# Block-sparse attention with a mixture of experts on one core: the first loads spread over two issuing engines

## The chip, the core and the metric

The kernel runs on one core of one Trainium2 chip. A core has five engines that run side by side, each with its own instruction queue in order: TensorE (PE in the profile, with PEld for its weight loads), VectorE (DVE), ScalarE (ACT), GpSimd (POOL) and SyncE (SP), which here issues loads and stores. Loads and stores (DMA) are carried out by 16 transfer engines; an issuing engine only starts them, and a semaphore tells the others when one has landed. The metric is the device time of one execution in microseconds (us). Three runs of the kernel before took 535.43, 535.45 and 536.15 us; the median is 535.45.

## The reference

The inputs are queries, keys and values of 4 batches, 8 heads, 768 positions and head dimension 64, in float32, and a list of three sampled key blocks for each of the 24 query blocks of 32 positions. Attention is masked by blocks, and its result goes through a mixture of 8 experts, one per token:

```python
scores = scale * np.matmul(q, k.transpose(0, 1, 3, 2))
mask = np.abs(blk_i - blk_j) <= 1
mask = mask | (blk_i == 0) | (blk_j == 0) | (blk_i == n_blocks - 1) | (blk_j == n_blocks - 1)
for qb in range(n_blocks):
    for kb in sampled_blocks[qb]:
        mask[qb * block:(qb + 1) * block, kb * block:(kb + 1) * block] = True
scores = np.where(mask, scores, -1000000000.0)
attn = softmax(scores)                      # maximum taken away, divided by the sum
x = (attn @ v), heads side by side          # 3072 tokens x 512
logits = x @ w_gate + modality_bias[modality_id]
e = argmax(logits);  out = softmax(logits)[e] * (relu(x @ w1[e]) @ w2[e])
```

## The kernel before, in words

The first and the last query block of every batch see all keys; this is the dense part (items `d`, by batch and pair of heads). The 22 blocks between see eight key blocks each: the two ends, three neighbours and three sampled ones; this is the sparse part (items `s`). Sampled blocks that repeat another one of the eight must be masked, so the list of blocks is turned into a table of masks (`smask`) first. In the second half of the program tokens are gathered by expert in groups of 256 and go through two matrix products each; that part is TensorE's.

All loads of the start are issued from SyncE, in the order of the code from line 164 on: the list of blocks (`blk_raw`, line 165, broadcast to all 128 partitions, 72 KB), the first half of the dense queries of batches 0 and 1 (`dense_q(0, 0, 4)`, lines 146 to 149, 128 KB), then the keys of batch 0 (`dense_k(0)`, lines 151 to 156) as three loads: half `c=0` in two pieces of 512 and 256 KB, half `c=1` in one of 768 KB. Then follow the other dense queries, half of the keys of batch 1, the values of batch 0 (`dense_v`), the other half of batch 1's keys, its values, and three small tables for the gate (lines 177 to 179).

TensorE first runs 56 products of constants (`WARM`, lines 207 to 209). ScalarE's first instruction in the code is an exponential of one column (line 214), which needs its function table.

From line 1347 on every engine's order is written out by hand. For the start it is the list `START` (lines 50 to 55); a token names an operation and an item. It begins

```python
blk SP16 S00 S01 M00 S02 M01 X00 T00 X01 M02 T01 M03 X02 A00 T02 X03 A01 T03 kl0 S10 S11 A02 ...
```

`blk` is GpSimd's copy of the list's low words (`block_ids`, line 212, writes `rb_i`). `SP16` puts 16 steps of the table work (`tables`, lines 240 to 274) into VectorE's queue; the first is the cast of `rb_i` (line 242), and each step uses the one before. `S` is the dense scores on TensorE (line 378; one call makes two head pairs, so `S01` adds nothing), `M` the row maxima on VectorE (lines 391 to 394), `X` the exponentials on ScalarE (lines 400 and 401), `T` the transposes on TensorE (line 410), `A` their copies out of PSUM (line 417, the first two on VectorE, the others on ScalarE), `W` the product with the values (lines 430 and 432), `O` the division (lines 446 to 451). So on VectorE the maxima of the first scores stand behind the 16 table steps.

For the first sparse items GpSimd copies key blocks out of the dense keys into a buffer (`share_k`, lines 461 to 481; the number of a sampled block is loaded from `rb_i` first, line 458), SyncE loads the group's queries (`fetch_q`, line 143), the numbers of its sampled blocks (line 512) and its values (`fetch_v` and `fetch_own`, lines 484 to 520). TensorE's sparse scores are line 532, VectorE's masking and maximum line 540.

Of the kernel before, what the change touches and what calls it, by code (L numbers as in the profile page):

```python
# [13 lines left out]
I32 = mybir.dt.int32  # L14
# [6 lines left out]
P = 128  # L21
# [67 lines left out]
def attention_moe(ctx, tc, kD, qD, qH, v0, v1, blocks, modality, w_gate, bias, w1, w2, out):  # L89
    nc = tc.nc  # L90
# [28 lines left out]
    with ExitStack() as actx:  # L119
# [9 lines left out]
        def slot(n, dt=F32):  # L129
            return big.tile([P, 3 * 1024 + 2], dt, name="slot", tag=f"slot{n}", bufs=1)  # L130
# [8 lines left out]
        qd = {}  # L139
# [3 lines left out]
            nc.sync.dma_start(q_raw.rearrange("p n f -> p (n f)"), qH[half, m])  # L143
            return q_raw.rearrange("p n (u q) -> p u n q", q=32)

        def dense_q(half, u0=0, u1=8):
            if half not in qd:
                qd[half] = work.tile([P, HB * NPAIR, 64], F32, name="qd", bufs=1)
            nc.sync.dma_start(qd[half][:, u0:u1].rearrange("p u q -> p (u q)"), qD[half][:, 64 * u0:64 * u1])

        def dense_k(b, cs=(0, 1), js=None):
            if b not in kd:
                kd[b] = slot(KD_SLOT[b])[:, 0:3072].rearrange("p (c j f) -> p c j f", c=2, j=NB)
            for c in cs:
                for j0, j1 in js or (((0, 16), (16, 24)) if (b, c) == (0, 0) else ((0, 24),)):
                    nc.sync.dma_start(kd[b][:, c, j0:j1, :].rearrange("p j f -> p (j f)"), kD[b, :, c, j0 * 64:j1 * 64])
# [5 lines left out]
                nc.sync.dma_start(vd[b][:, t:t + n, :], vH[b // HB][t * P:(t + n) * P, b % HB].rearrange("(t p) f -> p t f", p=P))  # L162

        blk_raw = const.tile([P, NB * 3 * 2], I32, name="blk_raw")
        nc.sync.dma_start(blk_raw, blocks.bitcast(I32).rearrange("a b -> (a b)").partition_broadcast(P))
        dense_q(0, 0, 4)
        wg_raw = const.tile([P, NPAIR, E], F32, name="wg_raw")
        mod_raw = const.tile([P, NT, 2], I32, name="mod_raw")
        b_raw = const.tile([P, 2, E], F32, name="b_raw")

        dense_k(0)
        dense_q(0, 4, 8)
        dense_k(1, (0,))
        dense_v(0)
# [1071 lines left out]

        spares.append(tables())
        side(Q_IN, lambda: dense_q(1))
        for b in (2, 3):
            for t in range(6):  # L1250
# [6 lines left out]
        for g in range(2 * NM):  # L1257
            half, m = divmod(g, NM)
# [185 lines left out]
```

## Time and profile before

| | |
|---|---|
| median of three runs | 535.45 us (535.43 to 536.15) |
| the profiled execution | 536.03 us |
| its span, first to last instruction | 534.3 us |
| mean granted TensorE clock in it | 0.987 |
| TensorE busy | 514.9 us, 96% |
| VectorE busy | 377.2 us, 71% |
| ScalarE busy | 335.2 us, 63% |
| GpSimd busy | 214.9 us, 40% |
| loads and stores | 119.44 MB, 224 GB/s on average |

How to read the rows that follow. In a timeline, a row has start and duration in us, engine (a "q" behind it marks its queue's own work, such as issuing a load), line of the code, operation, tiles written and read, shape, and a count of merged instructions; in brackets stand the idle time of the engine before it and what ended that. In the chain of waits, a row has start, duration and what the chain ran through. In a view of stretches, a row has the stretch, its length, busy time and instructions of each engine, TensorE's granted clock, the busy share of the transfer engines and GB/s. A row of waits has who waited for whom, total us, how often, and the longest. A row of loads has issuing engine, count, KB each and us from issue to landing. What releases an instruction is inferred from semaphores, so a wait on several is put down to the last one by the profile.

### The profile page before, as it was taken

How to read it: one execution, taken by the hardware profiler on the slowest of the kernel's cores; microseconds unless marked ns; L12 is line 12 of the kernel's file. 1: busy time of each engine (PE TensorE's matmuls, PEld its weight loads, DVE VectorE, ACT ScalarE, POOL GpSimd, SP SyncE). 2: the span in 40 equal slices, each digit the busy share in tenths (PEclk: the TensorE clock that was granted, in tenths of full speed). 3: DMA queues.
4: the chain of work that ended last, by engine and by line, in shares of the span. 5: the costliest groups of instructions: out<-in, count | busy, mean ns of one | idle time of the engine just before them, and what ended most of it. 6: DMA issues, size and time to landing. Idle time of an engine off the chain costs nothing.

```text
span 534.3 us, 19017 instructions
## 1 busy us (share of the span) xinstructions
PE 514.9 (96%) x7298; PEld 436.1 (82%) x7298; DVE 377.2 (71%) x1139; ACT 335.2 (63%) x765; POOL 214.9 (40%) x451
## 2 busy tenths in 40 slices
PE   7999999998999999899999999999999999999995
PEld 5667776766778777788989898998989899898984
DVE  7995698683788999867997656556565655656553
ACT  4689877884988878835456554546555454655552
POOL 3577685574468884323155022030302203030213
PEclk9999999997999999899999999999999999999998
DMA  7995887898846798965888686676758677675840
GB/s 278 339 234 153 238 244 224 243 229 223 232 126 194 198 231 252 274 193 200 238 288 303 227 261 200 237 252 202 244 177 261 203 227 242 213 246 180 257 155 23
DMA packets 49443, 119.44 MB, mean 224 GB/s; under 512 B 7744, under 2 KB 8128, under 8 KB 49344
## 3 DMA queue, kind: packets, MB, share of 16 engines
q1 hardware_dynamic: 45248, 105.02, 64.5%
q0 software_dynamic: 4096, 13.12, 7.3%
q8 instruction: 59, 0.97, 0.8%
q14 instruction: 40, 0.33, 0.2%
HBM read 105.52 MB, written 12.86 MB: 222 GB/s over the span
## 4 chain that ended last, share of the span: by engine, by line
issue 40%; PE 39%; DVE 7%; DMA 6%; POOL 6%; SPq 2%; ACT 1%; POOLq 0%; DVEq 0%; ACTq 0%
PE bank L557 7%; PE bank L532 6%; PE bank L579 4%; PE bank L588 4%; POOL slot L735 3%; DMA out<-slot,si 2%; DMA slot<-kD 2%; PE bank L605 2%; POOL out L789 2%; PE bank L595 2%; DVE y L540 2%; PE bank L753 1%; PE bank L769 1%; PE bank L770 1%; PE bank L768 1%
## 5 line engine op out<-in xcount | busy, mean ns | idle before, releaser
L724 DVE TENSOR_TENSOR slot<-slot 128x1024 fp32r<-128x1024 f32 x99 | 123.1, 1248 | 89.3 <-ACT slot L721 87.5
L721 ACT CAST slot<-slot 128x1024 fp32r<-128x1024 f32 x104 | 108.1, 1048 | 102.1 <-PE bank L754 52.1
L753 PE MATMUL bank<-slot 128*128 128x256 f32 x384 | 108.4, 282 | 0.0
L755 PE MATMUL bank<-slot 128*128 128x256 f32 x384 | 107.8, 281 | 0.0
L754 PE MATMUL bank<-slot 128*128 128x256 f32 x384 | 107.7, 280 | 0.0
L789 POOL DMA_INDIRECT out<-slot,si x20 | 25.4, 1270 | 178.6 <-ACT slot L785 175.6
L548 ACT ACTIVATE a<-y,mn 128x256 f32<-128x256 f32 x176 | 88.7, 511 | 7.7 <-DVE mn L540 7.6
L768 PE MATMUL bank<-slot 128*128 128x512 f32 x192 | 76.6, 399 | 0.0
L769 PE MATMUL bank<-slot 128*128 128x512 f32 x192 | 75.9, 395 | 0.0
L770 PE MATMUL bank<-slot 128*128 128x512 f32 x192 | 75.8, 395 | 0.0
L753 PEld LDWEIGHTS bank<-slot 128*128 128x128 f32 x384 | 72.3, 188 | 0.6
L754 PEld LDWEIGHTS bank<-slot 128*128 128x128 f32 x384 | 72.1, 188 | 0.4
L755 PEld LDWEIGHTS bank<-slot 128*128 128x128 f32 x384 | 72.2, 188 | 0.0
L540 DVE CUSTOM_DVE_ANT_1 y<-bank,smask 128x256 f32<-128x256 f32 x176 | 66.3, 416 | 0.6 <-PE bank L532 0.2
L481 POOL COPY slot<-slot 128x128 f32 x264 | 63.9, 294 | 0.0
L562 ACT COPY at<-bank 128x512 f32<-128x512 f32 x88 | 50.6, 576 | 12.8 <-PE bank L557 12.7
L557 PE MATMUL bank<-ident,a 128*128 128x128 f32 x352 | 52.8, 284 | 0.6 <-ACT a L400 0.5
L503 POOL TENSOR_SCALAR slot<-slot 32x1024 f32<-32x1024 f32 x40 | 41.9, 1048 | 28.0 <-PE bank L588 10.2
L532 PE MATMUL bank<-slot,q_raw 64*32 64x256 f32 x1408 | 48.8, 382 | 1.1 <-DMA q_raw<-qH 0.7
L770 PEld LDWEIGHTS bank<-slot 128*128 128x128 f32 x192 | 36.1, 188 | 8.4
L557 PEld LDWEIGHTS bank<-ident,a 128*128 128x128 f32 x352 | 38.9, 142 | 4.7 <-ACT a L548 0.8
L769 PEld LDWEIGHTS bank<-slot 128*128 128x128 f32 x192 | 36.1, 188 | 7.8 <-DVE slot L724 0.4
(302 smaller groups left out, 855.4 us busy)
## 6 DMA issues: line engine op xcount, KB each, us to landing
slot<-w SPq DMA_DIRECT2D x100, 512.0 KB, 4.0
slot<-v SPq DMA_DIRECT2D x180, 128.0 KB, 4.0
x_d<-xr SPq DMA_DIRECT2D x22, 256.5 KB, 5.3
q_raw<-qH SPq DMA_DIRECT2D x22, 256.0 KB, 4.8
slot<-v SPq DMA_DIRECT2D x16, 256.0 KB, 4.9
slot<-kD SPq DMA_DIRECT2D x13, 256.0 KB, 4.2
slot<-v SPq DMA_DIRECT2D x4, 768.0 KB, 11.9
slot<-w SPq DMA_DIRECT2D x10, 256.0 KB, 5.1
```

Source lines behind the costliest of these rows:

```text
L532: nc.tensor.matmul(sp[u][32 * pr:32 * pr + 32, b * 256:(b + 1) * 256], lhsT=q[r, b * NPAIR + pr, n, :], rhs=kv[r, s0:s0 + 8, b, pr, :], st ...
L540: nc.vector.tensor_tensor_reduce(y[:, u, :].rearrange("p (s f) -> p s f", s=8), sp[u][:, b * 256:(b + 1) * 256].rearrange("p (s f) -> p s ...
L548: nc.scalar.activation(a[:, u, :], y[:, u, :], AF.Exp, bias=mn[:, u:u + 1], scale=-1.0, accum_out=total[:, u:u + 1])
L557: nc.tensor.transpose(tp[:, k:k + P], a[:, u, c * P:(c + 1) * P], ident)
L721: nc.scalar.copy(h, s)
L724: (eng or (nc.gpsimd if n in POOL_SPLITS else nc.vector)).tensor_tensor(l, s, h.bitcast(F32), ALU.subtract)
L753: nc.tensor.matmul(o, lhsT=h[:, fs], rhs=xh[g % 2][:, c, :], start=c == 0 and f % 2 == 0, stop=False)
L754: nc.tensor.matmul(o, lhsT=h[:, fs], rhs=xl[g % 2][:, c, :], start=False, stop=False)
L755: nc.tensor.matmul(o, lhsT=l[:, fs], rhs=xh[g % 2][:, c, :], start=False, stop=c == 3 and f % 2 == 1)
L768: nc.tensor.matmul(o, lhsT=hh[0][:, f, ts_], rhs=h[:, fs], start=f == 0, stop=False)
L769: nc.tensor.matmul(o, lhsT=hh[0][:, f, ts_], rhs=l[:, fs], start=False, stop=False)
L770: nc.tensor.matmul(o, lhsT=hl[f // 4][:, f % 4, ts_], rhs=h[:, fs], start=False, stop=f == 7)
```

## The change

The first four dense query groups and the list of blocks are issued from ScalarE's queue, in this order, the list after the first half of the keys in the code. SyncE's first issue is the first piece of batch 0's keys, followed by the second piece, by half `c=1`, and by all that came after it before. Nothing else is changed: sizes, tiles and the order written out by hand stay.

```diff
-        def dense_q(half, u0=0, u1=8):
+        def dense_q(half, u0=0, u1=8, eng=nc.sync):
             if half not in qd:
                 qd[half] = work.tile([P, HB * NPAIR, 64], F32, name="qd", bufs=1)
-            nc.sync.dma_start(qd[half][:, u0:u1].rearrange("p u q -> p (u q)"), qD[half][:, 64 * u0:64 * u1])
+            eng.dma_start(qd[half][:, u0:u1].rearrange("p u q -> p (u q)"), qD[half][:, 64 * u0:64 * u1])
...
         blk_raw = const.tile([P, NB * 3 * 2], I32, name="blk_raw")
-        nc.sync.dma_start(blk_raw, blocks.bitcast(I32).rearrange("a b -> (a b)").partition_broadcast(P))
-        dense_q(0, 0, 4)
         wg_raw = const.tile([P, NPAIR, E], F32, name="wg_raw")
         mod_raw = const.tile([P, NT, 2], I32, name="mod_raw")
         b_raw = const.tile([P, 2, E], F32, name="b_raw")
 
-        dense_k(0)
+        dense_q(0, 0, 4, nc.scalar)
+        dense_k(0, (0,))
+        nc.scalar.dma_start(blk_raw, blocks.bitcast(I32).rearrange("a b -> (a b)").partition_broadcast(P))
+        dense_k(0, (1,))
         dense_q(0, 4, 8)
```

## The prediction

> **What bounds the kernel now.** I read the page first, then the chain of waits over the first 30 us, busy time by stretches, VectorE's waits, and the timeline of the first 25 us.
>
> ```profile
> span 534.3 us, 19017 instructions
> PE 514.9 (96%) x7298; PEld 436.1 (82%) x7298; DVE 377.2 (71%) x1139; ACT 335.2 (63%) x765; POOL 214.9 (40%) x451
> ```
>
> Over the span TensorE is the bound. But the change touches only the issues of the first two microseconds, so what counts is who sets the pace of the start, and whether a shift there lasts to the end. The chain of waits has one answer:
>
> ```profile
> 5.61 13.10 DMA slot<-kD
> ...
> 24.68 4.25 DMA slot<-v
> ...
> 29.41 1.10 DVE btmp L280
> ```
>
> Read so, SyncE's loads are the path: keys until 18.7, values until 28.9, then VectorE. Busy time in stretches speaks against it:
>
> ```profile
> core 0: us, PE busy (x) PEld busy (x) DVE busy (x) ACT busy (x) POOL busy (x), PEclk, DMA share, GB/s
> 4.26:40.40 36.14, 32.31 (x583) 22.79 (x581) 33.45 (x136) 24.34 (x79) 20.55 (x67) 1.00 0.98 306
> ```
>
> ```profile
> DVE rb L242 <- POOL rb_i L212: 0.4, 1, 0.4
> DVE nm L391 <- PE bank L378: 0.4, 1, 0.4
> DVE y L540 <- PE bank L532: 0.2, 1, 0.2
> ```
>
> From 4.26 to 40.40 us VectorE is busy 33.45 of 36.14 us, and these three are all its waits between 4 and 40 us; none is on a load of keys or values. I take the chain's step from a value load to VectorE's L280 for a wait put down to the wrong transfer: L280 computes with the bias, not with values. So VectorE, in its order written out by hand, paces the start, and the timeline shows what lets it begin:
>
> ```profile
> 0.81 0.40 SPq L165 DMA_DIRECT2D blk_raw<-blocks  x1
> 0.81 1.28 ACT L214 ACT_TABLE_LOAD   x1 [0.81 <-PEq L1437]
> 1.26 0.42 SPq L149 DMA_DIRECT2D qd<-qD  x1
> 1.73 1.37 SPq L156 DMA_DIRECT2D slot<-kD  x3
> 2.10 0.20 ACT L214 ACTIVATE gs<-onesb 128x1 f32<-128x1 bf16 x1
> 3.99 0.24 POOL L212 COPY rb_i<-blk_raw 128x72 int32<-128x72 int32 x1 [1.99 <-DMA blk_raw<-blocks]
> 4.26 0.20 DVE L242 CAST rb<-rb_i 128x72 f32<-128x72 int32 x1 [0.43 <-POOL rb_i L212]
> ...
> 6.23 1.52 PE L378 MATMUL bank<-slot,qd 64*64 64x512 f32 x16
> ...
> 7.85 0.19 DVE L268 TENSOR_TENSOR rm<-rm,t 128x24 f32<-128x24 f32 x1
> 7.96 0.69 DVE L391 TENSOR_REDUCE nm<-bank 128x1 f32<-128x512 f32 x1
> ...
> 9.10 1.52 PE L378 MATMUL bank<-slot,qd 64*64 64x512 f32 x16 [1.35 <-DMA slot<-kD]
> ...
> 9.25 1.15 POOL L469 TENSOR_SCALAR slot<-slot 128x256 f32<-128x256 f32 x3 [5.02 <-DMA slot<-kD]
> ...
> 9.32 0.69 ACT L400 ACTIVATE a<-bank,nb__263 128x512 f32<-128x512 f32 x1 [7.02 <-DVE nb__263 L394]
> ...
> 10.55 1.62 PE L410 MATMUL bank<-ident,a 128*128 128x128 f32 x12
> ...
> 14.52 0.21 PEld L378 LDWEIGHTS bank<-slot,qd 64*64 64x64 f32 x8 [0.17 <-DVE slot L417]
> ...
> 15.64 0.69 DVE L391 TENSOR_REDUCE nm<-bank 128x1 f32<-128x512 f32 x1 [0.41 <-PE bank L378]
> ...
> 23.84 1.10 PE L532 MATMUL bank<-slot,q_raw 64*32 64x256 f32 x32 [0.65 <-DMA q_raw<-qH]
> ```
>
> The list of blocks lands at about 3.9, GpSimd copies it at 3.99, VectorE starts its table work at 4.26 and is still in it when the first row maxima are due: L391 starts at 7.96, right behind L268 at 7.85, with no wait between. The scores for it were in at 6.23 + 1.52 = 7.75. ScalarE waits for that maximum (9.32), TensorE's transposes for ScalarE (10.55). The list of blocks, first on SyncE, opens the path; the keys do not.
>
> **The change part by part.** (1) *Keys earlier.* SyncE's list and query issues go, so its first key issue moves from 1.73 to 0.81: 0.92 us, and as much for everything behind it on SyncE. That is the most; it is worth nothing until the bound is reached. The first scores begin at 6.23, when TensorE's warm-up products end; nothing earlier is possible by keys. The wait of 1.35 us at 9.10 shrinks by up to 0.92, but its results are wanted only after two more sets of maxima, on a VectorE with no gap. GpSimd's key copies (9.25) and the 0.65 us wait at 23.84 come earlier beside VectorE. I count 0.
>
> (2) *Queries from ScalarE.* Issued at about 0.81 instead of 1.26; they are needed at 6.23. Count 0.
>
> (3) *ScalarE's own time.* Two issues of some 0.42 us, the price of such a one on SyncE, ahead of its table load: that then ends near 0.81 + 0.84 + 1.28 = 2.9 and L214 near 3.2. Nothing waits there: ScalarE idles for 7.02 us up to 9.32. Without that cover it would cost 0.84.
>
> (4) *The list of blocks, second on ScalarE.* Here is the price. Queued behind it: GpSimd's copy L212 and its loading of key numbers (which has the 5.02 us wait before 9.25 as cover), and VectorE's whole table work with everything after it. The landing in the new order is not in the trace; it is bounded by these, from issue to landing:
>
> ```profile
> blk_raw<-blocks SPq DMA_DIRECT2D x1, 72.0 KB, 3.1
> ```
>
> ```profile
> qd<-qD SPq DMA_DIRECT2D x1, 128.0 KB, 3.0
> ```
>
> ```profile
> slot<-kD SPq DMA_DIRECT2D x1, 256.0 KB, 4.6
> ```
>
> The list now lands at 0.81 + 3.1 = 3.9. Best case: it behaves as the queries do now, second on a queue with one small load ahead: 1.26 + 3.0 = 4.3, so 0.35 us later. Earlier than now is excluded: it was the first transfer of all, issued at the first possible moment. Worst case: it lands when the second piece of keys does. That piece is issued at 1.73 + 1.37/3 = 2.2 and lands at 6.8 today, 0.92 earlier then: 5.9, so 2.0 us later. Between: what shares the transfer engines with it in the new order is 128 KB of queries, 512 KB of keys and perhaps the next 256 KB, close to what lies ahead of that key piece today. These rows show how full the engines are with keys running:
>
> ```profile
> 3.00:3.50 0.50, 0.50 (x8) 0.50 (x6) 0.43 (x4) 0.00 (x0) 0.00 (x0) 1.00 0.50 105
> 3.50:4.00 0.50, 0.50 (x8) 0.50 (x6) 0.30 (x2) 0.00 (x0) 0.01 (x1) 1.00 0.98 258
> ```
>
> The second-last number is the share of transfer engines busy: half until 3.5, while only the small loads and the first keys move, 0.98 after it. With keys first the full load is there by the time the list's packets come. So the list is nearer the worst case; I take two thirds of the way, 0.35 + 0.65 x 1.65 = 1.4 us later. A rule bears on it: the Trainium skill, DMA: Bandwidth & Descriptors, Issuing engines are not separate DMA queues, says that loads issued from ScalarE and SyncE run on the same 16 engines and interleave, and that a second issuer saves only issue time. By it the list has no lane of its own; the sum does not use it.
>
> (5) *Does 1.4 us last?* VectorE has no slack before it: L391 stood right behind the table work. Behind it, the two gaps are 0.41 at 15.64 and 0.2. The first is ended by scores whose weight load waited for VectorE (14.52), so it moves along; at most the 0.6 of both is absorbed, and I absorb none. Then TensorE takes over:
>
> ```profile
> 36.76 1.10 PE L532 MATMUL bank<-slot,q_raw 64*32 64x256 f32 x32 [0.49 <-DVE xrd L451]
> ...
> 38.62 0.57 PE L579 MATMUL bank<-slot,at 128*64 128x64 f32 x12 [0.50 <-ACT at L562]
> ```
>
> ```profile
> 40.00:60.00 20.00, 19.61 (x548) 15.25 (x553) 12.45 (x63) 18.18 (x61) 14.52 (x39) 1.00 0.63 186
> ```
>
> It waits for VectorE and ScalarE at 36.76 and 38.62 and is then busy for 19.61 of 20 us, so it starts its own long stretch later by the same amount, and nothing after that runs by a clock from outside.
>
> The sum: 0 + 0 + 0 + 1.4. The profiled execution took 536.03 us (span 534.3 and 1.7 around it) and would take 537.4; it lies 0.6 above the median of the runs shown, 535.45, which becomes 536.85.
>
> **The rivals.** *The list is hardly later* (under 0.9 us): if packets of ScalarE's queue slip between the keys' large ones. For it: queries and list are small, 200 KB together. Against it: the 0.98 above. Price 0 to 0.9, about 535.9.
>
> *SyncE's queue is the path*, as the chain of waits has it. Then the keys, the group queries awaited at 23.84 and the values of 28.9 all come 0.92 earlier: 534.5. It decides if the list lands by about 4.3, so that VectorE stays ahead of its inputs. Against it: VectorE's busy 33.45 us leaves hardly that much to gain.
>
> *The change doesn't do what it says*: ScalarE loads its table first, so both issues wait until 2.1. The list is then issued 1.28 us later than reckoned and lands between 5.6 and 7.2; at 6.4 that is 2.5 late: 537.95. Against it: the load stands right ahead of L214 now, and belongs to it.
>
> *A stall elsewhere moves.* TensorE once ran dry for no reason the profile shows, and its clock was halved afterwards:
>
> ```profile
> 121.60 0.69 PE L579 MATMUL bank<-slot,at 128*64 128x64 f32 x8 [2.65 <-issue]
> ```
>
> ```profile
> 117.52:120.93 3.41, 1.43 (x47) 0.88 (x31) 3.41 (x20) 2.56 (x9) 3.25 (x5) 1.00 0.96 219
> 120.93:127.76 6.83, 6.16 (x49) 4.50 (x53) 0.35 (x3) 3.16 (x10) 3.65 (x15) 0.50 1.02 265
> ```
>
> The gap cost 2.65 and the clock of 0.50 half of 6.16: 5.7 together. Other timing of transfers could remove it (529.7) or add one. The same clock is a risk in the start: under my forecast TensorE ends its second scores near 9.10 + 1.52 - 0.92 = 9.7 and waits until 10.55 + 1.4 = 11.95, idle 2.2 us. At 0.50 for 3.4 us it could lose 1.7, partly under VectorE; I put half, 0.85, into the upper end. The Trainium skill, TensorE: Matmul & The Clock Gate, Part 1: The HAM clock gate, asks a whole idle window of about 3.4 us for a halving, so by it there would be none; the 2.65 us gap here was shorter and the clock fell, so the trace differs.
>
> **How the numbers follow.** About 0.2%, 1.07 us, is what a measurement of this kernel can tell from no change. Forecast (list 0.9 to 2.0 late) 0.50, of which 0.43 lies beyond that bound; hardly later 0.20; SyncE's path 0.12, whose 0.92 lies just inside the bound (0.07 within, 0.05 beyond); table first 0.08; a stall moved 0.10, half each way. Slower: 0.43 + 0.08 + 0.05 = 0.56. Same: 0.07 + 0.20 + 0.07 = 0.34. Faster: 0.05 + 0.05 = 0.10. The range goes up to 535.45 + 2.0 + 0.85 = 538.3 and down to 535.0, which takes in the late list with absorption and the neutral case, and leaves out most of SyncE's path.
>
> **What would show it.** Right: L212 near 5.4, L242 near 5.7, L391 near 9.4 and the first exponential near 10.7, while the keys' wait at 9.10 falls toward 8.2; VectorE without a gap until about 42. Wrong: L242 at 4.6 or before; or L242 late and VectorE's later gaps growing so that L579 at 38.62 stays where it is; or a first ScalarE issue behind the table load.

## The result and the profile after

| | before | after |
|---|---|---|
| median of 22 runs each, same chip | 535.93 us | 541.17 us |
| ratio after to before, with its 95% interval | | 1.0072 (1.0049 to 1.0096) |
| the profiled execution | 536.03 us | 541.20 us |
| its span | 534.3 us | 539.5 us |
| mean granted TensorE clock in it | 0.987 | 0.988 |

The kernel became slower: the interval says by 2.6 to 5.1 us (0.0049 and 0.0096 of 535.9). The forecast was 536.85 with a range of 535.0 to 538.3; the sign was right, the size was not. The ratios here and below leave disturbed runs out, so a ratio need not be the quotient of two medians; for e5 and e8 so many were left out that it says little there, and their traces are what is read; the profiled executions of e1 and e8 are themselves among those left out.

Lines of the code are one higher after the change from the loads on (L242 is now L243, L391 is L392, L532 is L533). The page of after begins:

```profile
span 539.5 us, 19017 instructions
...
PE 515.8 (96%) x7298; PEld 436.2 (81%) x7298; DVE 379.6 (70%) x1139; ACT 335.5 (62%) x765; POOL 215.7 (40%) x451
```

TensorE has the same work, 515.8 for 514.9 us, in a span 5.2 us longer: it waits more. The timeline of after, cut to the rows that answer to those shown of before:

```profile
0.80 1.34 SPq L156 DMA_DIRECT2D slot<-kD  x3
...
0.81 0.40 ACTq L149 DMA_DIRECT2D qd<-qD  x1
...
1.24 0.46 ACTq L171 DMA_DIRECT2D blk_raw<-blocks  x1
...
1.73 1.28 ACT L215 ACT_TABLE_LOAD   x1 [1.73 <-PEq L1438]
...
7.11 0.24 POOL L213 COPY rb_i<-blk_raw 128x72 int32<-128x72 int32 x1 [5.12 <-DMA blk_raw<-blocks]
7.39 0.20 DVE L243 CAST rb<-rb_i 128x72 f32<-128x72 int32 x1 [3.56 <-POOL rb_i L213]
...
9.04 1.52 PE L379 MATMUL bank<-slot,qd 64*64 64x512 f32 x16 [1.43 <-DMA slot<-kD]
...
11.53 0.68 DVE L392 TENSOR_REDUCE nm<-bank 128x1 f32<-128x512 f32 x1
...
12.89 0.69 ACT L401 ACTIVATE a<-bank,nb__263 128x512 f32<-128x512 f32 x1 [9.66 <-DVE nb__263 L395]
...
13.81 0.84 PE L411 MATMUL bank<-ident,a 128*128 128x128 f32 x6 [3.25 <-ACT a L401]
...
19.80 0.69 DVE L392 TENSOR_REDUCE nm<-bank 128x1 f32<-128x512 f32 x1 [0.81 <-PE bank L379]
```

ScalarE issues first and loads its table afterwards (1.73). The list is copied at 7.11 where it was 3.99. VectorE's cast, the first step of its table work, starts at 7.39 and had been at 4.26: 3.13 us late. The row maxima stand right behind the table work as before and come 3.57 late (11.53 for 7.96), the exponential 3.57 (12.89 for 9.32), the transposes 3.26 (13.81 for 10.55). The second product of keys hardly moved: 9.04 for 9.10. The loads of after that were issued in the first 3 us, with KB and us from issue to landing:

```profile
slot<-kD SPq DMA_DIRECT2D x1, 512.0 KB, 4.3
slot<-kD SPq DMA_DIRECT2D x1, 256.0 KB, 5.0
qd<-qD ACTq DMA_DIRECT2D x1, 128.0 KB, 4.5
...
blk_raw<-blocks ACTq DMA_DIRECT2D x1, 72.0 KB, 5.8
```

The list took 5.8 us from issue to landing where it had taken 3.1, and the queries ahead of it on ScalarE's queue took 4.5 where they had taken 3.0. The second key piece takes 5.0 for 4.6: 0.4 of the 0.9 us by which it was issued earlier is given back under way. The chain of waits now names the list by itself (start, us, what):

```profile
1.24 5.81 DMA blk_raw<-blocks
7.11 0.25 POOL rb_i L213
7.39 0.21 DVE rb L243
7.62 0.24 DVE t L247
```

VectorE's waits in after between 2 and 43 us (total, times, longest) are again few:

```profile
DVE rb L243 <- POOL rb_i L213: 3.6, 1, 3.6
DVE nm L392 <- PE bank L379: 0.8, 1, 0.8
```

Once it has the list it runs without a gap but for one of 0.81 us, which was 0.41. So the lateness is carried by VectorE's own work, as the prediction had it, and it can be followed to TensorE. The third sparse scores of TensorE (L533, at 36.76 before) and the products behind them (at 38.62 before) stand in the timeline of after at

```profile
40.01 1.09 PE L533 MATMUL bank<-slot,q_raw 64*32 64x256 f32 x32
41.04 0.33 PE L580 MATMUL bank<-slot,at 128*64 128x64 f32 x2
41.55 1.15 PE L580 MATMUL bank<-slot,at 128*64 128x64 f32 x30 [0.18 <-ACT at L563]
```

that is 3.25 and 2.93 us later. This place, the 36.76 of before, is used below as the mark of what the start costs. At 61.08 of before the shift is 2.81.

Behind that, the two profiled executions part by another 2 us in single stalls of TensorE that no other engine ends. In after the largest and one more are

```profile
105.79 0.39 PE L433 MATMUL bank<-slot 128*64 128x64 f32 x6 [1.87 <-issue]
...
222.63 0.43 PE L589 MATMUL bank<-slot,at 128*32 128x64 f32 x16 [3.24 <-issue]
```

and before had 2.65 at 121.60 and

```profile
218.07 0.43 PE L588 MATMUL bank<-slot,at 128*32 128x64 f32 x16 [1.83 <-issue]
```

Their size changes from one execution to the next: a second profile of the kernel before (e12) had 2.38 at 124.37 and 0.99 at 219.29 and ended 2.2 us later than the first. The start's 2.8 to 3.3 us alone lies within the measured 2.6 to 5.1. Whether the change also makes such stalls likelier stays open.

### The profile page after: what moved, and what is told of

It is laid out like the page before. It is cut to its first block, busy times and chain, and to the rows that moved or that the text cites. A ratio compares the mean times of both kernels' runs of the same rounds, so it can differ in the third digit from the quotient of the medians.

```text
span 539.5 us, 19017 instructions
## 1 busy us (share of the span) xinstructions
PE 515.8 (96%) x7298; PEld 436.2 (81%) x7298; DVE 379.6 (70%) x1139; ACT 335.5 (62%) x765; POOL 215.7 (40%) x451
## 4 chain that ended last, share of the span: by engine, by line
issue 40%; PE 38%; DVE 8%; POOL 6%; DMA 4%; SPq 2%; ACT 1%; POOLq 1%; ACTq 0%; DVEq 0%
PE bank L533 6%; PE bank L558 6%; PE bank L580 3%; PE bank L589 3%; DMA out<-slot,si 2%; POOL slot L736 2%; PE bank L606 2%; PE bank L411 2%; POOL out L790 2%; PE bank L596 2%; PE bank L433 2%; PE bank L754 1%; PE bank L770 1%; PE bank L771 1%; PE bank L769 1%
## 5 line engine op out<-in xcount | busy, mean ns | idle before, releaser
L533 PE MATMUL bank<-slot,q_raw 64*32 64x256 f32 x1408 | 50.2, 387 | 0.3 <-issue 0.2
```

What stands on the lines that cost most here:

```text
L533: nc.tensor.matmul(sp[u][32 * pr:32 * pr + 32, b * 256:(b + 1) * 256], lhsT=q[r, b * NPAIR + pr, n, :], rhs=kv[r, s0:s0 + 8, b, pr, :], st ...
```

## The experiments

Fifteen kernels were run. The main theory, A in the expectations, is the prediction's own: the landing of the list sets the moment at which VectorE starts, and this lasts. Its rivals: the loads from SyncE set the start; TensorE's halved clock behind its longer idle time makes up the cost; and, on why the list is so late, that bytes issued ahead of it delay it whatever queue it is on, or that ScalarE's queue itself is the slow one. Where a text splits A or gives another letter, it is one of these. Diffs are against after, unless said otherwise. For each run two rows of its timeline are read: the cast (7.39 in after, 4.26 before) and the third sparse scores (40.01 and 36.76). The expectations name TensorE's instructions at 57 us instead (57.16 in before); read there, the shifts differ from those given below by 0.6 us at most. The medians of the kernel before, beside which the runs stand, were 536.62 (e1 to e4), 538.46 (e5 to e8), 537.82 (e9 to e11) and 539.31 us (e12 to e15).

### VectorE alone made late: e5

Against the kernel before, with its loads untouched; the copies rewrite a constant with the same values:

```diff
+            for _ in range(14):
+                nc.vector.tensor_copy(iota_f, iota_i)
             nc.vector.tensor_copy(rb, rb_i.rearrange("p (n t) -> p n t", t=3))
```

> The kernel before, with no load touched; VectorE alone makes 14 more copies of iota_f (some 0.23 us each, 3.2 us) ahead of its cast of the list, as long as the list is late in the changed kernel. Theory A (a late start of VectorE is the cost, whatever makes it late): TensorE's instructions at 57 us come 2.5 to 3.3 us later than before, and the time is 2.5 to 5 us over before, like the changed kernel. Theory C (the second queue, or SyncE's waits, is the cost): within 1 us of before.

```profile
4.13 0.24 POOL L212 COPY rb_i<-blk_raw 128x72 int32<-128x72 int32 x1 [2.13 <-DMA blk_raw<-blocks]
...
7.29 0.19 DVE L244 CAST rb<-rb_i 128x72 f32<-128x72 int32 x1
```

```profile
40.26 1.09 PE L534 MATMUL bank<-slot,q_raw 64*32 64x256 f32 x32
```

The list is in as early as before (4.13), only VectorE is late: 3.03 us at the cast, 3.50 at the scores. That is the picture of after (3.13 and 3.25) with no load touched. By time the run is unclear: the ratio, 1.0016 (0.9970 to 1.0062), takes in no change and ends just short of the 0.65% that 3.50 us would be. Late VectorE work alone is enough to make the shift in the trace. It brings TensorE's halved clock with it (0.50 from 15.0 to 18.4), so e5 doesn't tell these two apart.

### VectorE freed of the table work: e7 and e8

All the table work (16 steps and the rest, L242 to L273 of before) is moved from VectorE to GpSimd, in before (e7) and in after (e8):

```diff
-            nc.vector.tensor_copy(rb, rb_i.rearrange("p (n t) -> p n t", t=3))
+            nc.gpsimd.tensor_copy(rb, rb_i.rearrange("p (n t) -> p n t", t=3))
...
-            nc.vector.tensor_tensor(rm, rm, t0, ALU.add)
+            nc.gpsimd.tensor_tensor(rm, rm, t0, ALU.add)
...
```

> The kernel before with the table work on the list moved from VectorE to GpSimd, which idles from 4.2 to 9.3 us. Theory A (VectorE paces the start): VectorE is freed of 3.7 us between 4.26 and 7.96; TensorE's instructions at 57 us come 1 to 3 us earlier, where loads set in as the next bound (the values awaited at 16.8, the queries at 23.84); time 1 to 3 us under before. If SyncE's loads pace the start (the rival of the prediction): no change.

> The changed kernel with the same move of the table work to GpSimd, so that VectorE no longer waits for the list at first. Theory A: the late list stops costing; TensorE's instructions at 57 us within 0.7 us of those of the kernel before with the same move, and the time within 0.2% of it, 3 to 6 us under the changed kernel. Theory C: it stays 3 us or more behind the kernel before with the same move.

The scores in e7 and then, with the cast on GpSimd, e8:

```profile
36.65 1.10 PE L532 MATMUL bank<-slot,q_raw 64*32 64x256 f32 x32 [0.49 <-DVE xrd L451]
```

```profile
7.39 0.24 POOL L243 CAST rb<-rb_i 128x72 f32<-128x72 int32 x1
```

```profile
36.94 1.10 PE L533 MATMUL bank<-slot,q_raw 64*32 64x256 f32 x32 [0.36 <-DVE xrd L452]
```

In e8 the list is as late as in after, yet the scores are 0.18 us behind those of before instead of 3.25: it is VectorE's order behind the list that carries the lateness. The times say less: e8 has stalls of up to 2.38 us later on in its profiled execution, and a ratio of 0.9984 (0.9936 to 1.0032). e7 was the miss of the group: it took 4 us of work off VectorE (29.43 us busy from 4.26 to 40.40 for 33.45), and the scores came 0.11 earlier where 1 to 3 were expected; ratio 1.0033 (0.9996 to 1.0070). Its VectorE waits for TensorE's first scores until 7.25, only 0.71 before its first maximum in before, and another 2.1 us for scores until 28.90. Its TensorE waits 1.3 us for keys at 8.96, as it did in before, and 1.17 for the group queries at about 24, where before waited 0.65. So TensorE's first scores and the loads stand right behind VectorE as a second bound: the start of before can be made later by VectorE, but not much earlier by it alone.

### The table work moved behind: e4

```diff
-blk SP16 S00 S01 M00 S02 M01 X00 T00 X01 M02 T01 M03 X02 A00 T02 X03 A01 T03 kl0 ...
+blk S00 S01 M00 S02 M01 X00 T00 X01 M02 T01 M03 X02 A00 T02 X03 A01 SP16 T03 kl0 ...
```

> Changed kernel, but VectorE's 16 table steps stand behind the row maxima and copies of the first dense items in the hand-written order, so that the late list no longer holds up the first maxima (they start at about 7.7 instead of 11.5) nor TensorE's transposes. Theory A (VectorE is busy without a gap from its start to 40 us, so what counts is when it starts its unbroken work): it starts at 7.7 instead of 7.39, so nothing comes back; shift at 57 us still 2.5 to 3.3, time as the changed kernel within 0.2%. Theory B (TensorE's idle stretch and halved clock): both are gone, and the shift at 57 us falls to 0 to 1.

```profile
7.30 0.69 DVE L392 TENSOR_REDUCE nm<-bank 128x1 f32<-128x512 f32 x1 [3.47 <-PE bank L379]
...
14.62 0.19 DVE L243 CAST rb<-rb_i 128x72 f32<-128x72 int32 x1
```

```profile
39.55 1.09 PE L533 MATMUL bank<-slot,q_raw 64*32 64x256 f32 x32
```

VectorE now waits for scores instead of the list and starts at 7.30, 3.04 us after the 4.26 of before; the scores come 2.79 late. Median 538.46, ratio 1.0063 (1.0028 to 1.0097). Reordering doesn't help: what was lost is VectorE's time before 7.3, and the work has to be done sooner or later. The halved clock was expected to go, but it only moved: TensorE now idles 2.82 us up to 20.95 and runs at 0.50 from 22.5 on, so this run doesn't rule the clock out.

### TensorE's clock: e6

The stretches of after show what follows TensorE's idle time of 3.25 us (columns as in the prediction; the last but two is the granted clock):

```profile
10.50:14.00 3.50, 0.25 (x6) 0.22 (x3) 3.29 (x12) 1.11 (x4) 1.31 (x6) 1.00 1.05 397
...
15.05:18.46 3.41, 3.41 (x17) 3.14 (x16) 3.30 (x11) 3.37 (x12) 1.14 (x4) 0.50 1.02 390
```

e6 puts 56 products of constants ahead of the first transposes:

```diff
-blk SP16 S00 S01 M00 S02 M01 X00 T00 ...
+blk SP16 S00 S01 M00 S02 M01 X00 fill T00 ...
...
+        def keep_busy():
+            spin = bank()
+            for _ in range(56):
+                nc.tensor.matmul(spin[:, 0:P], lhsT=onesb, rhs=onesb, start=True, stop=True)
```

> Changed kernel with 56 more products of constants on TensorE between the second dense scores and the first transposes, about 3.1 us at full clock, where it idles for 3.25 us. Theory A: the halved clock of 15.0 to 18.5 us goes, but the shift at 57 us stays within 0.7 of the changed kernel's 2.8. Theory B (the halved clock behind the idle stretch is most of the cost): the shift falls to 0 to 1.3.

```profile
13.76 3.29 PE L1259 MATMUL bank<-onesb 128*128 128x128 bf16 x56 [3.18 <-ACT a L401]
16.89 2.79 PE L411 MATMUL bank<-ident,a 128*128 128x128 f32 x24
```

```profile
40.90 1.09 PE L533 MATMUL bank<-slot,q_raw 64*32 64x256 f32 x32
```

By the profile the products waited for ScalarE's exponential, which reads a bank of PSUM, and so ran behind the idle time, not in it; as a fill it failed. But the clock stayed at 1.00 this time, and the 24 transposes took 2.79 us, where after spends 0.84 and 3.90 on the same 24. With the clock whole, and 3.29 us of extra work in the way, the scores are 0.89 us later than in after; ratio 1.0104 (1.0051 to 1.0158). Neither expectation came true, and the run doesn't separate the two effects. What bounds the halved clock in after is VectorE's one wait for TensorE: 0.81 us there, 0.41 in before, and 0.41 to 0.42 in e2, e3 and e11 below, whose lists are late too but whose clock stays at 1.00. By 28.97 TensorE is waiting again, 0.80 us for ScalarE, so nothing of its slow stretch is left over. The halving cost the path about 0.4 us, not three.

### Why the list is late: order and queue, e1, e2, e3, e9, e11

All five move only loads. e1 swaps the two on ScalarE, the list first:

```diff
-        dense_q(0, 0, 4, nc.scalar)
-        dense_k(0, (0,))
         nc.scalar.dma_start(blk_raw, blocks.bitcast(I32).rearrange("a b -> (a b)").partition_broadcast(P))
+        dense_k(0, (0,))
+        dense_q(0, 0, 4, nc.scalar)
```

e2 has the list first on SyncE and only the queries on ScalarE:

```diff
+        nc.sync.dma_start(blk_raw, blocks.bitcast(I32).rearrange("a b -> (a b)").partition_broadcast(P))
         dense_q(0, 0, 4, nc.scalar)
         dense_k(0, (0,))
-        nc.scalar.dma_start(blk_raw, blocks.bitcast(I32).rearrange("a b -> (a b)").partition_broadcast(P))
```

e3 leaves the list alone on ScalarE, with the queries ahead of the keys on SyncE:

```diff
-        dense_q(0, 0, 4, nc.scalar)
-        dense_k(0, (0,))
         nc.scalar.dma_start(blk_raw, blocks.bitcast(I32).rearrange("a b -> (a b)").partition_broadcast(P))
+        dense_q(0, 0, 4)
+        dense_k(0, (0,))
```

e9 keeps the order of after but issues everything from SyncE, so that the list is fourth, behind a key piece, the queries and the other key piece:

```diff
-        dense_q(0, 0, 4, nc.scalar)
-        dense_k(0, (0,))
-        nc.scalar.dma_start(blk_raw, blocks.bitcast(I32).rearrange("a b -> (a b)").partition_broadcast(P))
+        dense_k(0, (0,), ((0, 16),))
+        dense_q(0, 0, 4)
+        dense_k(0, (0,), ((16, 24),))
+        nc.sync.dma_start(blk_raw, blocks.bitcast(I32).rearrange("a b -> (a b)").partition_broadcast(P))
```

e11 does the same with the list first, then a key piece, the queries and the other key piece:

```diff
-        dense_q(0, 0, 4, nc.scalar)
-        dense_k(0, (0,))
-        nc.scalar.dma_start(blk_raw, blocks.bitcast(I32).rearrange("a b -> (a b)").partition_broadcast(P))
+        nc.sync.dma_start(blk_raw, blocks.bitcast(I32).rearrange("a b -> (a b)").partition_broadcast(P))
+        dense_k(0, (0,), ((0, 16),))
+        dense_q(0, 0, 4)
+        dense_k(0, (0,), ((16, 24),))
```

> Changed kernel, but on ScalarE the list of blocks is issued first and the queries second. Theory A (the landing of the list sets when VectorE starts, and that shift lasts): the list now alternates with the first key piece only and lands at about 5.0 to 5.4 (the queries, first on ScalarE, landed at 5.30 in the changed kernel), VectorE's cast of it starts near 5.5 instead of 4.26 before and 7.39 after; TensorE's instructions at 57 us come 1.0 to 1.3 us later than before, and the time is 1 to 1.5 us over before. Theory B (the cost is TensorE's idle stretch of 3.25 us and the halved clock behind it at 15 us): the idle stretch falls to about 1.5 us, no halved clock in the first 20 us, no lasting shift. Theory C (a second issuing queue as such, with SyncE's issues waiting for its transfers, is the cost): as slow as the changed kernel, about 5 us over before.

> The list stays SyncE's first load, the queries go to ScalarE, the keys follow the list on SyncE. Theory A: the list lands at 3.9 to 4.2, VectorE's cast starts at 4.2 to 4.6, TensorE's instructions at 57 us within 0.4 us of before; time within 0.2% of before, and nothing is gained though the keys are issued 0.45 us earlier than before. Theory B: no long idle stretch, as before. Theory C: still slower than before by a good part of the 5 us, because ScalarE's queue is in use.

> Only the list goes to ScalarE's queue; SyncE issues the queries first and then the keys. Theory A: the list shares the engines with the queries' small packets at first and lands at 3.8 to 4.6; VectorE's cast at 4.1 to 4.9, shift at 57 us 0 to 0.6, time within 0.2% of before. Theory C: slower than before by several us.

> The changed kernel's order of loads (keys, queries, second key piece, list, rest of the keys), but all of it on SyncE's one queue. If the list is late in the changed kernel because some 900 KB are ahead of it on the transfer engines (theory A1), it lands at 6.6 to 7.1 here as well (the fourth load of the kernel before landed at 6.84, of the changed kernel's list at 7.06) and VectorE's cast starts at 6.9 to 7.4; shift at 57 us 2.3 to 3.3. If the second queue itself delays it (theory A2: packets of the two queues held up by each other), it lands well under 6.4 here.

> All on SyncE: list, first key piece, queries, second key piece, the rest; that is the kernel before with the first key piece and the queries exchanged, so keys are first after the list and nothing is on ScalarE. Theory A: the list lands at 3.9 as before, VectorE's cast starts at 4.2 to 4.4, shift at 57 us within 0.4, time within 0.3% of before: earlier keys gain nothing. If keys set the pace: 0.4 us or more faster at 57 us.

GpSimd's copy, which starts when the list has landed, in e1, e2, e11 and e9, and the issue in e9:

```profile
6.37 0.24 POOL L213 COPY rb_i<-blk_raw 128x72 int32<-128x72 int32 x1 [4.37 <-DMA blk_raw<-blocks]
```

```profile
5.30 0.24 POOL L213 COPY rb_i<-blk_raw 128x72 int32<-128x72 int32 x1 [3.30 <-DMA blk_raw<-blocks]
```

```profile
5.42 0.24 POOL L214 COPY rb_i<-blk_raw 128x72 int32<-128x72 int32 x1 [3.42 <-DMA blk_raw<-blocks]
```

```profile
2.19 0.43 SPq L172 DMA_DIRECT2D blk_raw<-blocks  x1
...
8.76 0.24 POOL L214 COPY rb_i<-blk_raw 128x72 int32<-128x72 int32 x1 [6.75 <-DMA blk_raw<-blocks]
```

| run | list issued by, place | copy | cast | scores later than before | ratio |
|---|---|---|---|---|---|
| before | SyncE, first, queries next | 3.99 | 4.26 | 0 | 1 |
| e2 | SyncE, first, keys next | 5.30 | 5.58 | 0.54 | 1.0005 (0.9967 to 1.0043) |
| e11 | SyncE, first, keys next | 5.42 | 5.70 | 0.54 | 0.9996 (0.9955 to 1.0036) |
| e3 | ScalarE, alone | 5.84 | 6.11 | 1.44 | 1.0038 (1.0004 to 1.0073) |
| e1 | ScalarE, first | 6.37 | 6.64 | 3.14 | 1.0026 (0.9982 to 1.0069) |
| after | ScalarE, second | 7.11 | 7.39 | 3.25 | 1.0072 (1.0049 to 1.0096) |
| e9 | SyncE, fourth, behind two key pieces | 8.76 | 9.03 | 4.49 | 1.0102 (1.0068 to 1.0136) |

Most of these missed what was expected of them: e2, e3 and e11 were to have the cast at 4.1 to 4.9, as if keys behind the list or beside it cost little, and for e9 both theories had the list at 7.1 at the latest. Three things follow. A later cast goes with later scores, though not one for one: e1's cast is 0.75 earlier than that of after and its scores 0.11; VectorE's wait for TensorE at half clock is 1.12 us there, 0.81 in after. The second queue is not needed to make the list slow: behind the keys on SyncE's own queue (e9) it is slower still. And the list's place in its queue is not all either: e11 issues it at the same moment as before and only sends keys right behind it, where before sends the small queries first, and that costs 1.43 us (5.42 for 3.99). In e1 the list is issued at 0.80 and takes until 6.37, with the keys issued at the same moment from the other queue; about 5.5 was expected at the cast, and it was 6.64. So the keys' packets beside those of the list matter, not only bytes ahead of them.

### Why the list is slow beside keys: e10, e13, e14, e15

e10 loads the first half of the keys in one load of 768 KB instead of 512 and 256:

```diff
-        dense_k(0, (0,))
+        dense_k(0, (0,), ((0, 24),))
```

> The changed kernel with the first half of the keys in one load of 768 KB (128 packets of 6 KB) instead of two of 512 and 256 KB (packets of 4 and 2 KB). The same bytes are issued ahead of the list. Theory A1 (bytes issued ahead of it): the list lands at 7.0 to 7.4 as in the changed kernel (7.06). Theory A2 (each engine takes a packet of one queue and one of the other in turn, so each of ScalarE's small packets waits for one of SyncE's large ones): the queries' 8 packets per engine pair with 8 of 6 KB, the list's with 8 of the next 6 KB load, 8 x (0.234 + 0.046) + 8 x (0.234 + 0.029) = 4.3 us instead of 2.5; the list lands at 8.4 to 9.2, VectorE's cast starts at 8.7 to 9.5 and the shift at 57 us is 4 to 5.

```profile
9.48 0.24 POOL L213 COPY rb_i<-blk_raw 128x72 int32<-128x72 int32 x1 [7.48 <-DMA blk_raw<-blocks]
```

```profile
42.70 1.09 PE L533 MATMUL bank<-slot,q_raw 64*32 64x256 f32 x32
```

The list, issued at the same 1.24 on the same queue, is ready 2.4 us later than in after. The keys' bytes come in the same order, but a row of them goes as one larger packet instead of two, and with one issue less the next 768 KB are issued some 0.45 us earlier. I read it so: the packets of ScalarE's queue take turns with the keys', and the size of those sets their pace. The cast, at 9.75, is later still than the 9.5 that this theory allowed. The scores are 5.94 us behind before; ratio 1.0076 (1.0033 to 1.0118).

The other three replace the broadcast. In the kernels so far all 128 partitions read the same 576 bytes of memory. Here the input holds the list 128 times, one row for each partition; the bytes written are the same. e13 does so in after, e14 in before, e15 in e11:

```diff
-        nc.scalar.dma_start(blk_raw, blocks.bitcast(I32).rearrange("a b -> (a b)").partition_broadcast(P))
+        nc.scalar.dma_start(blk_raw, blocks.bitcast(I32))
...
-        "blocks": np.ascontiguousarray(inputs["sampled_blocks"]),
+        "blocks": np.ascontiguousarray(np.broadcast_to(np.asarray(inputs["sampled_blocks"]).reshape(1, NB * 3), (P, NB * 3))),
```

e12, the kernel before once more, stands beside them.

> The kernel before, unchanged, for a second profile. All theories: the list lands at 3.8 to 4.1 and VectorE's cast starts at 4.1 to 4.4, if the landing of 3.93 in the first profile is the rule and not luck; TensorE's instructions at 57 us within 0.4 us of the first profile's.

> The changed kernel, but the list of blocks lies 128 times in memory, one row per partition, so that its 128 packets read 128 places instead of the same 576 bytes. Theory A3 (reading one place 128 times is slow as soon as key packets run beside it): the list lands at 5.5 to 6.3, VectorE's cast starts at 5.8 to 6.6, shift at 57 us 1 to 2.2. Theory A1/A2 (packets and bytes ahead of it, or the turns of the two queues): as in the changed kernel, landing 6.9 to 7.2, cast 7.2 to 7.5, shift 2.4 to 3.2.

> The kernel before with the list laid out 128 times in the same way. Theory A3: little to win where hardly any key packets run beside the list: landing 3.3 to 4.0, cast 3.7 to 4.3, time within 0.3% of before. Theory A1/A2: the same.

> List first on SyncE, then the first key piece, then queries, with the list laid out 128 times. Without that layout the list's packets ran until 5.01 and VectorE's cast started at 5.70, against 3.62 and 4.26 in the kernel before, with the list in the same first place. Theory A3: packets end by 4.0, cast 4.0 to 4.6. Theory A1/A2: still near 5.0 and 5.7, since what runs beside it is the same.

The copies of e12, e13, e14 and e15, in this order:

```profile
4.12 0.24 POOL L212 COPY rb_i<-blk_raw 128x72 int32<-128x72 int32 x1 [2.12 <-DMA blk_raw<-blocks]
```

```profile
6.22 0.24 POOL L213 COPY rb_i<-blk_raw 128x72 int32<-128x72 int32 x1 [4.23 <-DMA blk_raw<-blocks]
```

```profile
2.86 0.24 POOL L212 COPY rb_i<-blk_raw 128x72 int32<-128x72 int32 x1 [0.86 <-DMA blk_raw<-blocks]
```

```profile
2.77 0.24 POOL L214 COPY rb_i<-blk_raw 128x72 int32<-128x72 int32 x1 [0.78 <-DMA blk_raw<-blocks]
```

With a row for each partition the list is ready 2.65 us earlier beside keys (2.77 for 5.42, e15 against e11), 1.26 earlier in the order of before (2.86 for 4.12) and 0.89 earlier in after (6.22 for 7.11). In e15 the keys right behind the list cost it nothing any more.

The traces also hold a record of every packet, and those of the list are told by their size, 576 bytes; each run has 128 of them. The start of the first and the end of the last:

| run | list's packets, us | length |
|---|---|---|
| before | 1.83 to 3.62 | 1.79 |
| e11 | 1.84 to 5.01 | 3.17 |
| e15, rows | 1.82 to 2.36 | 0.54 |
| e1 | 2.81 to 6.00 | 3.19 |
| after | 4.43 to 6.75 | 2.32 |
| e13, rows | 4.41 to 5.70 | 1.29 |
| e10 | 5.30 to 8.95 | 3.65 |
| e9 | 4.72 to 8.36 | 3.64 |

This splits the 3.13 us of after: the list's packets begin 2.60 us later than in before and then run 0.53 longer. The late begin is spent behind the queries, which are ahead on ScalarE's queue: their 128 packets run from 2.34 to 4.81 (2.31 to 3.96 in before), beside the 128 of the first key piece, from 1.85 to 4.72. Rows change nothing in that (4.41 in e13). In e10 the keys' first 128 packets, now of 6 KB, run until 5.24, the queries until 5.57, and the list begins at 5.30. So the small packets of one queue end with the large ones of the other, as they would if the queues took turns packet by packet. The broadcast read is the larger part where the list meets keys from the start (3.17 us for 0.54), and the smaller one in after (2.32 for 1.29). Why 128 reads of one place are slow was not measured, but the transfer engines are not full meanwhile. From 5.0 to 6.5 us, in after and then in e13 (the last but one is the busy share of the transfer engines):

```profile
5.00:6.50 1.50, 1.50 (x25) 1.20 (x26) 0.00 (x0) 0.00 (x0) 0.00 (x0) 1.00 0.56 166
```

```profile
5.00:6.50 1.50, 1.50 (x17) 1.50 (x15) 0.00 (x1) 0.00 (x0) 0.24 (x1) 1.00 1.06 422
```

The scores stand 0.18 (e12), 2.21 (e13), -0.57 (e14) and 0.39 us (e15) from those of before. Times: e12 538.26 and e15 540.80, one run each; e13 540.29, ratio 1.0050 (1.0013 to 1.0088); e14 537.43, ratio 0.9965 (0.9921 to 1.0009). e14 has the lowest ratio of all, but its interval takes in no change. In it, VectorE starts at 3.74 without waiting for the list at all, so an earlier list can't start it more than 0.52 us sooner than in before.

## Why the prediction was wrong in size, by its steps

**Step 1, keys.** Counted at 0: right in the sum. Of the 0.92 us by which the keys were issued earlier, 0.06 arrived (9.04 for 9.10). The second scores need half `c=1` of the keys; the last of its 128 packets of 6 KB ends at 8.35 in before, at 8.48 in after and at 7.54 in e13, so the gain was lost while the broadcast list was under way, with the engines 0.56 busy. That the earlier keys would show as a shorter wait at 9.10 was wrong, and so was the idle time of 2.2 us that was reckoned from it for TensorE's clock: it was 3.25. e2 and e11 also issue keys earlier and gain nothing.

**Steps 2 and 3, queries and ScalarE's time.** Both 0, right: the first scores begin at 6.09 for 6.23, and ScalarE has 9.66 us of idle time behind the issues. The rival of a table load ahead of the issues is refuted (1.73, behind both).

**Step 4, the list.** This is the step that failed. It put the list 1.4 us later, with 2.0 at worst; it was 3.13 at the cast. The worst case was tied to the second key piece, which was to land at 5.9; that piece in fact lands at about 6.3 (issued near 1.25, 5.0 under way), and the list later than it, at 1.24 + 5.8 = 7.0. The step took the queries ahead of the list for a small load, as in the 3.0 us of before, and the list's 72 KB for a size like any other. The runs showed two terms that it lacked. The first is the wait behind the queries: beside keys these took 4.5 us, and the list's packets began 2.60 us late, most of the 3.13. That the queries are so slow because the two queues take turns packet by packet is a reading, which e10 bears out (2.4 us more for keys in larger packets). The second is the broadcast: reading one place 128 times is slow beside keys (e15 against e11: 2.65 us; e13 against after: 0.89). The row of the list's 3.1 us in before was measured with no keys ahead; it could not bound what it does among them. Nor were the engines full, the reason given for two thirds of the way: they were 0.56 busy from 5.0 to 6.5. The rule that the prediction cited, in the Trainium skill, DMA: Bandwidth & Descriptors, Issuing engines are not separate DMA queues, says that a second issuer saves only issue time. That the list gets no lane of its own agrees with the 5.8 us. Whether only issue time is saved stays open: e9 issues the list 0.95 us later than after (2.19 for 1.24), and its packets begin 0.29 later (4.72 for 4.43), but they run longer there, and it is ready 1.65 later (8.76 for 7.11).

**Step 5, whether it lasts.** Right in the mechanism, as e5 and e8 show: VectorE's start sets the start of the rest. In detail the lateness first grew and then shrank. Between the cast and the maxima it grew by 0.44, as table steps ran beside GpSimd's work at 9.24 to 10.4 and took 0.30 to 0.34 us where before has 0.19 to 0.20. In after, two of them, and the first operation again 1.3 us later:

```profile
9.39 0.30 DVE L263 TENSOR_TENSOR t<-rb 128x24 f32<-128x24 f32 x1
9.72 0.34 DVE L265 TENSOR_TENSOR t<-t 128x24 f32<-128x24 f32 x1
...
10.71 0.20 DVE L263 TENSOR_TENSOR t<-rb 128x24 f32<-128x24 f32 x1
```

At the maxima of 19.80 it was 4.16 (15.64 before), the grown wait of 0.81 included; and by 40.01 it was 3.25: of TensorE's waits of before, 0.65 for the group queries at 23.84 and 0.49 for VectorE at 36.76 are gone, and one of 0.80 at 28.97 is new. Which step gave back how much was not taken apart. "I absorb none" was in any case too strict, by 0.8 to 0.9: e2 and e11, whose cast was 1.32 and 1.44 late, just the forecast's lateness, show 0.54 at the scores and no change in time. Had step 4 been right, step 5 would have made the forecast too slow.

**Rivals.** The list hardly later, and SyncE's queue as the path: both refuted, the first by 3.13, the second by e5, which changes no load; e7 shows the loads only as part of the next bound, at about the same time. A stall elsewhere: it did move, and makes the last 2 us between the two profiles, as above; that is not shown to come from the change. The clock risk in the start came true (0.50 from 15.05 to 18.46); its cost, about 0.4 as worked out under e6, lies within the 0.85 that the range allowed for it.

## What to carry to other kernels

The first small load can be the one that opens the path even if the chain of waits shows large ones: look at what the busiest engine waits for before its first long stretch without a gap, and keep that load free of large ones beside it and of others ahead of it on its queue. Price a moved load from a row where it runs among the same neighbours; a duration from an empty start is no bound. A small list broadcast to all partitions is worth laying out once for each partition if it has to share the engines with large packets.

## What the runs showed of the hardware

- A broadcast load of 576 bytes to 128 partitions was ready at 5.42 us with keys right behind it, and at 2.77 us as 128 rows of their own, issued at the same 0.80 us. While the broadcast was under way in after, the transfer engines were 0.56 busy (5.0 to 6.5 us); with rows, in e13, 1.06.
- A 72 KB load second on ScalarE's queue sent its first packet at 4.43 us, when most of the 128 small packets ahead of it were through; these ended at 4.81, the 128 larger key packets on SyncE's queue at 4.72.
- The granted clock fell to 0.50 after an idle time of TensorE of 3.25 us in after, and after 2.26 us in e1; in e6, after 3.18 us and then products of constants, it did not, nor in e9 after 2.39 us at 10.65. The Trainium skill, TensorE: Matmul & The Clock Gate, Part 1: The HAM clock gate, asks a whole idle window of about 3.4 us; the 2.26 us speaks against that as the only condition.
- Single TensorE stalls that nothing in the profile ends differ between executions of the same code (2.65 at 121.60 and 1.83 at 218.07 us in before, 2.38 at 124.37 and 0.99 at 219.29 in e12, up to 3.24 in after), and are nearly as large as the effect studied here.
